# Attention with a decaying complex state and a capacity-limited expert layer: small copies given to GpSimd, constants and first loads placed anew, attention's order planned anew

## The chip, the cores and the metric

One core of a Trainium2 chip runs the whole program. The metric is device time in microseconds (us) from the start of an execution to its end; below it is the median of three runs. The engines are PE (TensorE), DVE (VectorE), ACT (ScalarE), POOL (GpSimd) and SP (SyncE, which here only issues DMA transfers); PEld is PE's weight load.

## The reference

Two layers follow each other. The first is attention with a recurrent state for 4 batches x 8 heads, 768 positions and 48 features; the second sends each of the 3072 tokens to one of 8 experts, 384 tokens each, in the order of the largest logits.

```python
mag = np.sqrt(a_re * a_re + a_im * a_im)
scale = np.minimum(mag, 0.999) / (mag + 1e-06)
a_re_n, a_im_n = (a_re * scale, a_im * scale)
for t in range(S):
    ar, ai = (a_re_n[:, :, t, :, None], a_im_n[:, :, t, :, None])
    new_re = ar * S_re - ai * S_im
    new_im = ar * S_im + ai * S_re
    kv = np.einsum('bhd,bhe->bhde', k[:, :, t], v[:, :, t])
    S_re, S_im = (new_re + kv, new_im)
    y[:, :, t] = np.einsum('bhd,bhde->bhe', q[:, :, t], S_re)
...
logits = x @ w_gate
order = np.argsort(-flat)          # (token, expert) pairs, best first
...                                # a token goes to the first expert that has room
h = np.maximum(x[mask] @ w1[e], 0.0)
out[mask] = h @ w2[e]
```

## The kernel before

**Attention** works on 24 tiles of 128 positions (4 batches x 6). Three tiles make a group; there are 8 groups. The first group is cut into pieces of one and two tiles, the last into pieces of two and one, so that elementwise work on them can begin and end with less data.

For each group `elementwise` turns the decay factors into amounts that a plain product can use. Its stages have short names: F1 and F2 square the real part `ar` and the imaginary part `ai` on ACT, F3 forms `p` from both on DVE, F6 adds the squares on DVE, F5 to F11 take logarithms and exponentials on ACT and products on DVE, S scans the log-magnitude on DVE, G1 and G2 take its exponentials on ACT, G3 and G5 scale `kq` (keys and queries) with them on DVE. A1 and A2 give the angle on ACT, N0 sums it on DVE, T1, T2 and T3 make sine and cosine `CS` on ACT. G4 copies the last column of each tile into `gc` (the gate).

For each tile, `turns` then makes P0 (a copy of that tile's gate from `gc` into column 256 of tile buffer `f`), RQ (on DVE: `f<-kq,CS`, the rotation), and K (six transfers from SP's queue that restack `f` into `KQ`). K waits for both RQ and P0. There are four `f` buffers, so P0 of tile i also waits until K of tile i - 4 has read its buffer, and five `KQ` buffers.

`unit` is the rest of a tile: `kp` turns keys over (PE) and `kt` is its copy (ACT), `sc` are the scores (PE), `am` the masked scores (DVE), `U` the update of the state (PE), `W` the state carried on (DVE), `y` the output (PE), `xT` its copy (ACT), `xp` its turning (PE), `x` the copy of that (ACT), `lg` the logits (DVE). XS stores `x` to DRAM from POOL's queue, for the last two tiles from ACT's. There are two buffers of `x`.

**Fillers.** The table `FILL` gives for each tile a number of matmuls of no use (`sc<-mask,f`), issued ahead of that tile's scores once RQ of the tile is done. Their result is overwritten.

**What sets the order.** Every step is entered with `op` as engine, a cost in us, a priority and what it depends on. `in_order` is a planner in the program: it plays these steps through with one clock per engine and gives out the order of the instructions. Priorities are the tile's number plus an offset by kind of step from the table `OFF`. The class `Queue` then ties the instructions of each engine in that order, so engines run in order, and each waits where the result it needs is late. What is recorded through `Queue` shows as L138 in the profile (one helper line); L279 is ACT's load of a table of functions.

**Constants** are issued ahead of attention, not through `Queue`, so that DVE's constants (`ident`, `mask` at L61 and L62, two copies into `pick` at L83) may stand anywhere between its other instructions. Seven steps `later` (constants of the router, all made by POOL) are entered as DVE steps of 0.87 us each.

**After attention** `Router` and `experts` choose tokens by bisection of a threshold, gather them and run the experts' matmuls (`acc`). This part of the program isn't edited.

Of the kernel before, what the change touches and what calls it, by code (L numbers as in the profile page):

```python
# [15 lines left out]
OP = mybir.AluOpType  # L16
# [34 lines left out]
def constants(nc, con, z, w_gate):  # L51
    v, g = nc.vector, nc.gpsimd

    def t(n, shape, dt=F32):
        x = con.tile(shape, dt, name=n)
        setattr(z, n, x)
        return x

    jp = t("jp", [128, 128], I32)
    g.iota(jp, pattern=[[1, 128]], base=0, channel_multiplier=-1)  # L60
    v.tensor_scalar(t("ident", [128, 128]), jp, 0.0, None, op0=OP.is_equal)  # L61
    v.tensor_scalar(t("mask", [128, 128]), jp, 0.0, None, op0=OP.is_ge)  # L62
# [12 lines left out]
    t("wd", [128, 8])  # L75
    t("cidx", [128, NT])
    t("cidx2", [128, NT, 2], BF)
    t("pid", [128, 1])
    pick = t("pick", [128, 4, 112])
    v.memset(pick, 0.0)  # L80
    for s in range(2):
        r = slice(64 * s, 64 * s + 48)
        v.tensor_copy(pick[r, :, 48 * s:48 * s + 48], z.ident[r, None, r].to_broadcast([48, 4, 48]))  # L83
        g.dma_start(pick[r, :, 96:104], w_gate[:, s].rearrange("p d e -> d p e"))
    for s in range(2):
        r = slice(64 * s, 64 * s + 48)
        g.tensor_scalar(pick[r, :, 104:112], pick[r, :, 96:104], -1.0, None, op0=OP.mult)
    t("lg2", [128, NT + 1, 2, E])
    z.lg = z.lg2[:, :NT, 0]
    t("top", [128, NT])  # L90
    t("qm", [128, NT])
    t("oh", [128, NT, E], BF)
    t("ext", [128, 2])
# [164 lines left out]
def attention(nc, real, tc, z, kq_in, a_re, a_im, v_tok, xd, later):  # L258
    ctx = ExitStack()
    con = ctx.enter_context(tc.tile_pool(name="acon", bufs=1))  # L260
# [5 lines left out]
    v, g = nc.vector, nc.gpsimd  # L266
# [15 lines left out]
    act = nc.scalar.activation  # L282
# [52 lines left out]
    def free(name, stages, gi):  # L335
        return [x for s in stages for x in last_of(s, gi - BUFS[name])]
# [4 lines left out]
    def load_a(gi, j, name, src):  # L341
        b, c0, n = GROUPS[gi]
        lo, hi = cuts[gi][j]
        w = slice(lo * 128, hi * 128)
        return lambda: nc.sync.dma_start(
            get(name, gi, p=ld, bufs=1)[:, :, w], src[b, c0 // GC, :, :, w])

    def load_kq(gi):
# [15 lines left out]
    def elementwise(gi, j, at):  # L364
        b, c0, _ = GROUPS[gi]
        lo, hi = cuts[gi][j]
        n = hi - lo
# [10 lines left out]
        def add(stage, eng, cost, fn, deps):  # L378
            op((stage, gi, j), eng, cost, at, fn, deps)
# [2 lines left out]
            return [(s_, gi, j) for s_ in ss]  # L382

        first = -60.0 + 30.0 * j if gi == 0 else at
        op(("li", gi, j), "dma", 0.6, first, load_a(gi, j, "ai", a_im), free("ai", ["F2", "F3"], gi))
        op(("la", gi, j), "dma", 0.6, first, load_a(gi, j, "ar", a_re), free("ar", ["F1", "F3", "F4"], gi))
        for x in ops[-2:]:
            moved(x, 128 * (1 if n == GC else 3), 12 * T if n == GC else 512 * n)
# [24 lines left out]
        for c in range(n):  # L413
# [7 lines left out]
        add("G2", "act", sca(N3), lambda: act(G_("zi"), G_("zi"), AF.Exp), k_("G1"))  # L421
        add("G3", "dve", dve(N3), lambda: v.tensor_tensor(part(1), part(1), G_("s2").rearrange("p j (c t) -> p c j t", c=n), op=OP.mult),
            k_("G1") + [("lk", gi)])
        add("G4", "dve", 0.075, lambda: v.tensor_copy(
            get("gc", gi, [128, 3, GC], bufs=3)[:, :, lo:hi], G_("s2")[:, :, 127::128]), k_("G1") + free("gc", ["P0"], gi))
        add("G5", "dve", dve(N3), lambda: v.tensor_tensor(part(0), part(0), G_("zi").rearrange("p j (c t) -> p c j t", c=n), op=OP.mult),
            k_("G2") + [("lk", gi)])
# [25 lines left out]
    def turns(i):  # L453
# [8 lines left out]
        def ftile():  # L462
            return tiles["f", i]

        f_free = [("K", i - F_BUFS), ("FI", i - F_BUFS, len(FILL.get(i - F_BUFS, ())) - 1)] if i >= F_BUFS else []
        op(("P0", i), "dve", 0.07, i, lambda: v.tensor_copy(
            ftile()[..., 256], tiles["gc", gi][:, :, c, None].to_broadcast([128, 3, 2])), X("G4") + f_free)
        def rot():
            v.tensor_tensor(ftile()[..., :256].rearrange("p j s (m t) -> p (j s) m t", m=2),
# [159 lines left out]
            load(("lv", gi + 2), 0.6, elementwise_at + 4, load_v(gi + 2),  # L629
                 [("MX", gi * GC + c) for c in range(GC)] + [("ST", gi * GC + c) for c in range(GC)])  # L630
    for n, fn in enumerate(later):
        op(("later", n), "dve", 0.87, NT - 1.0, lambda fn=fn: fn(nc), [("later", n - 1)])

    def choices():
        r = slice(0, NT - 6)
# [46 lines left out]
class Router:  # L682
# [772 lines left out]

# [34 lines left out]
```

## Time and profile before

| what | us |
|---|---|
| median of 3 runs | 508.01 (507.87 to 508.49) |
| the profiled execution, its own time | 503.52 |
| its span, first to last instruction | 501.7 |
| attention: first RQ on DVE starts | 32.34 |
| attention: last `xp` on PE ends | 227.53 |
| PE busy, DVE busy, ACT busy, POOL busy over the span | 447.2, 391.7, 305.6, 113.8 |

The profile comes from one execution; times of rows count from the start of its span. Its own time is 1.8 us longer than its span and 4.5 us shorter than the median of the timed runs. A matmul's end is modelled, so that PE's busy time says that it had something in its queue, not that it ran at its peak. A row with "x8" merges eight equal instructions that follow each other; the time from the start of a row to the start of the next on the same engine is what an instruction costs its engine where no gap is named.

### The profile page before, as it was taken

How to read it: one execution, taken by the hardware profiler on the slowest of the kernel's cores; microseconds unless marked ns; L12 is line 12 of the kernel's file. 1: busy time of each engine (PE TensorE's matmuls, PEld its weight loads, DVE VectorE, ACT ScalarE, POOL GpSimd, SP SyncE). 2: the span in 40 equal slices, each digit the busy share in tenths (PEclk: the TensorE clock that was granted, in tenths of full speed). 3: DMA queues.
4: the chain of work that ended last, by engine and by line, in shares of the span. 5: the costliest groups of instructions: out<-in, count | busy, mean ns of one | idle time of the engine just before them, and what ended most of it. 6: DMA issues, size and time to landing. Idle time of an engine off the chain costs nothing.

```text
span 501.7 us, 9765 instructions
## 1 busy us (share of the span) xinstructions
PE 447.2 (89%) x3659; PEld 385.0 (77%) x3659; DVE 391.7 (78%) x1039; ACT 305.6 (61%) x577; POOL 113.8 (23%) x193
## 2 busy tenths in 40 slices
PE   0029999999999999995489999999999999999996
PEld 0017887888888989994365578898988988999995
DVE  6999999999999999836737778598896978925150
ACT  6999998987998949521033736364473743734241
POOL 8830000000010000012121324150331413830102
PEclk9999999999999999996599999999999999999998
DMA  7718687786879863621352515471170615750001
GB/s 263 303 36 238 196 286 226 240 252 208 253 231 241 249 172 100 168 86 49 127 172 80 220 48 173 159 272 44 54 293 33 258 73 202 286 174 16 33 17 47
DMA packets 37199, 82.51 MB, mean 164 GB/s; under 512 B 4352, under 2 KB 29184, under 8 KB 34080
## 3 DMA queue, kind: packets, MB, share of 16 engines
q1 hardware_dynamic: 30016, 42.55, 28.1%
q0 software_dynamic: 6848, 38.95, 21.3%
q8 instruction: 29, 0.48, 0.4%
q10 hardware_dynamic: 288, 0.39, 0.2%
q14 instruction: 18, 0.15, 0.1%
HBM read 53.49 MB, written 9.44 MB: 125 GB/s over the span
## 4 chain that ended last, share of the span: by engine, by line
PE 52%; DVE 17%; ACT 12%; issue 11%; DMA 4%; POOL 1%; SPq 1%; POOLq 1%; DVEq 0%; ACTq 0%
PE acc L138 35%; ACT s L138 5%; DVE f L138 4%; PE y L138 4%; PE sc L138 4%; PE cnt L138 4%; PE U L138 3%; DVE zi L138 2%; DMA ai<-in_a_im 2%; DVE neg L138 2%; DVE am L138 2%; PE xp L138 2%; DVE p L138 2%; ACT p L138 2%; ACT L279 2%
## 5 line engine op out<-in xcount | busy, mean ns | idle before, releaser
L138 ACT ACTIVATE hh<-acc 128x384 fp32r<-128x384 f32 (+1 forms) x64 | 31.3, 490 | 61.9 <-PE acc L138 54.0
L138 PE MATMUL sc<-mask,f 128*128 128x512 bf16 x126 | 32.4, 398 | 34.1 <-DVE f L138 34.1
L138 ACT ACTIVATE comp<-cnt 32x8 f16<-32x8 f32 (+1 forms) x144 | 24.3, 169 | 57.6 <-PE cnt L138 50.9
L138 PE MATMUL acc<-w2l,hh 128*128 128x384 f32 x168 | 56.7, 350 | 0.0
L138 PE MATMUL acc<-w2h,hl 128*128 128x384 f32 x168 | 56.3, 349 | 0.0
L138 PE MATMUL acc<-w2h,hh 128*128 128x384 f32 x168 | 55.3, 346 | 0.0
L138 PE MATMUL acc<-xh,w1h 128*128 128x384 f32 x168 | 55.0, 347 | 0.0
L138 PE MATMUL acc<-xh,w1l 128*128 128x384 f32 x168 | 54.8, 347 | 0.0
L138 PE MATMUL acc<-xl,w1h 128*128 128x384 f32 x168 | 54.5, 345 | 0.0
L138 POOL DMA_DIRECT2D xd<-x x22 | 12.2, 558 | 182.6 <-ACT x L138 182.5
L138 PEld LDWEIGHTS sc<-KQ 96*128 96x128 f32 x384 | 46.6, 192 | 4.5 <-issue 2.0
L138 PEld LDWEIGHTS <-f 128*128 128x128 bf16 x126 | 12.8, 103 | 48.0 <-DVE f L138 34.1
L138 PE MATMUL sc<-KQ 96*128 96x128 f32 x384 | 48.6, 277 | 0.0
L138 POOL DMA_INDIRECT out<-ot,idx x24 | 24.6, 1026 | 105.3 <-ACT ot L138 97.4
L138 DVE SCALAR_TENSOR_TENSOR hl<-acc,hh 128x384 fp32r<-128x384 f32 x56 | 30.6, 551 | 19.5 <-ACT hh L138 18.7
L138 DVE TENSOR_TENSOR f<-kq,CS 128x1536 f32<-128x1536 f32 x24 | 41.5, 1747 | 0.0
L138 DVE TENSOR_TENSOR ind<-m,thr 128x768 bf16<-128x768 f32 (+1 forms) x45 | 33.9, 771 | 8.5 <-PE thr L138 8.4
L138 POOL DMA_INDIRECT xg<-xd,idx x24 | 30.8, 1283 | 32.2 <-DVE idx L138 12.0
L138 PE MATMUL y<-am,V 128*64 128x128 f32 x384 | 36.5, 278 | 0.0
L138 DVE TENSOR_TENSOR am<-sc,mask 128x512 f32<-128x512 f32 x48 | 31.5, 681 | 5.6 <-PE sc L138 5.6
L138 PEld LDWEIGHTS acc<-w2l,hh 128*128 128x128 f32 x168 | 31.5, 189 | 0.8
L138 PEld LDWEIGHTS acc<-w2h,hl 128*128 128x128 f32 x168 | 31.3, 189 | 0.7 <-issue 0.3
(211 smaller groups left out, 1150.2 us busy)
## 6 DMA issues: line engine op xcount, KB each, us to landing
KQ<-f SPq DMA_DIRECT2D x144, 128.5 KB, 3.0
kq<-in_kq SPq DMA_DIRECT2D x8, 1152.0 KB, 6.6
V<-in_v SPq DMA_DIRECT2D x8, 576.0 KB, 7.5
xd<-x POOLq DMA_DIRECT2D x22, 192.0 KB
ar<-in_a_re SPq DMA_DIRECT2D x6, 576.0 KB, 3.9
ai<-in_a_im SPq DMA_DIRECT2D x6, 576.0 KB, 5.4
ar<-in_a_re SPq DMA_DIRECT2D x2, 384.0 KB, 4.0
ai<-in_a_im SPq DMA_DIRECT2D x2, 384.0 KB, 5.3
```

The source lines that it names most:

```text
L138: r = f(*a, **k)
L279: real.scalar.add_instruction(ins)
```

## The change

- G4 and P0, 10 and 24 small copies, are issued to POOL and no longer to DVE. The planner is given 0.45 and 0.75 us for them.
- The seven `later` steps are entered as POOL steps with costs of their own.
- Constants go through `Queue`, so they stand ahead of the first pieces on DVE. The two negations in `pick` move into the router's constants.
- The first group's two loads of `ai` are issued from ACT's queue; the loads of `ar` stay on SP's.
- `START`, `OFF` and `FILL` have new numbers, and the order comes out anew.

```diff
@@ constants
     for s in range(2):
         r = slice(64 * s, 64 * s + 48)
         v.tensor_copy(pick[r, :, 48 * s:48 * s + 48], z.ident[r, None, r].to_broadcast([48, 4, 48]))
         g.dma_start(pick[r, :, 96:104], w_gate[:, s].rearrange("p d e -> d p e"))
-    for s in range(2):
-        r = slice(64 * s, 64 * s + 48)
-        g.tensor_scalar(pick[r, :, 104:112], pick[r, :, 96:104], -1.0, None, op0=OP.mult)
@@ load_a
-        return lambda: nc.sync.dma_start(
+        q = nc.scalar if gi == 0 and name == "ai" else nc.sync
+        return lambda: q.dma_start(
             get(name, gi, p=ld, bufs=1)[:, :, w], src[b, c0 // GC, :, :, w])
@@ elementwise
-        op(("li", gi, j), "dma", 0.6, first, load_a(gi, j, "ai", a_im), free("ai", ["F2", "F3"], gi))
+        op(("li", gi, j), "dma" if gi else "act", 0.6, first - (0 if gi else 2000.0), load_a(gi, j, "ai", a_im), free("ai", ["F2", "F3"], gi))
...
-        add("G4", "dve", 0.075, lambda: v.tensor_copy(
+        add("G4", "pool", 0.45, lambda: g.tensor_copy(
             get("gc", gi, [128, 3, GC], bufs=3)[:, :, lo:hi], G_("s2")[:, :, 127::128]), k_("G1") + free("gc", ["P0"], gi))
@@ turns
-        op(("P0", i), "dve", 0.07, i, lambda: v.tensor_copy(
+        op(("P0", i), "pool", 0.75, i, lambda: g.tensor_copy(
             ftile()[..., 256], tiles["gc", gi][:, :, c, None].to_broadcast([128, 3, 2])), X("G4") + f_free)
@@ attention
-        op(("later", n), "dve", 0.87, NT - 1.0, lambda fn=fn: fn(nc), [("later", n - 1)])
+        op(("later", n), "pool", LATER[n], NT - 1.0, lambda fn=fn: fn(nc), [("later", n - 1)])
...
-START = dict(pe=0.0, act=0.6, dve=1.5, pool=3.4, dma=0.65)
+LATER = [3.3, 6.7] + [2.8] * 5
+START = dict(pe=0.0, act=0.3, dve=2.6, pool=4.3, dma=0.65)
...
-FILL = {0: (6, 6, 6), 1: (2, 2, 2), 3: (6, 6, 6), 4: (3, 3, 3), 5: (2, 2, 2), 6: (5, 5, 5), 7: (2, 2, 2), 8: (4, 4, 4), 9: (4, 4, 4), 11: (1, 1, 1), 12: (4, 4, 4), 14: (1, 1, 1), 18: (2, 2, 2)}
+FILL = {0: (6, 6, 6), 1: (2, 2, 2), 2: (4, 4, 4), 3: (2, 2, 2), 5: (6, 6, 6), 7: (4, 4, 4), 8: (1, 1, 1), 9: (3, 3, 3), 10: (1, 1, 1), 11: (3, 3, 3), 12: (3, 3, 3), 13: (2, 2, 2)}
@@ Router.masks
+        for s in range(2):
+            r = slice(64 * s, 64 * s + 48)
+            g.tensor_scalar(z.pick[r, :, 104:112], z.pick[r, :, 96:104], -1.0, None, op0=OP.mult)
@@ the program
-    constants(nc, con, z, w_gate)
+    queue = Queue(tc, nc, CHAIN)
+    constants(queue, con, z, w_gate)
     router = Router(nc, z, con)
-    queue = Queue(tc, nc, CHAIN)
```

`FILL` sums to 126 matmuls before and 111 now.

**The front, on DVE.** DVE's rows around its constants, before (`s_217` holds squares, `s_209` the real part's, `gc` and `f_119` are the gate copies of tile 0):

```order
L138 TENSOR_TENSOR s_217<-s_217,s_209 128x3x256
L61 TENSOR_SCALAR ident<-jp 128x128
L62 TENSOR_SCALAR mask<-jp 128x128
L83 COPY pick<-ident 48x4x48 x2
L138 TENSOR_TENSOR p<-p,s_209 128x3x128
L138 SCALAR_TENSOR_TENSOR zi<-zi,s_217 128x128 x3
L138 TENSOR_SCALAR zi<-s_217 128x3x256
L138 COPY gc<-s_217 128x3
L138 COPY f_119<-gc 128x6
```

The start of DVE's queue now:

```order
L135 TENSOR_SCALAR ident<-jp 128x128
L135 TENSOR_SCALAR mask<-jp 128x128
L135 MEMSET cb 128x1 x5
L135 MEMSET pick 128x448
L135 COPY pick<-ident 48x4x48 x2
L135 TENSOR_SCALAR neg<-ar 128x3x128
L135 SCALAR_TENSOR_TENSOR p<-ar,ai 128x3x128
```

The constants moved ahead of the first instruction that needs loaded data, and the copies left DVE. (The helper line is L135 in the changed program.)

**The front, on ACT.** ACT's rows up to the sines and cosines of the first group, before. The piece of one tile is 128x3x128, the piece of two 128x3x256; `CS<-p` is T3, `CS<-neg` T1, `p<-neg` T2; rows of 128x1152 belong to later groups:

```order
L138 ACTIVATE p<-neg 128x3x256
L138 ACTIVATE zi<-zi 128x3x256
L138 ACTIVATE s_280<-s_280,cb 128x1152
L279 ACT_TABLE_LOAD
L138 ACTIVATE CS<-p,cb 128x3x128
L138 ACTIVATE CS<-p,cb 128x3x256
L138 ACTIVATE CS<-neg 128x3x128
L138 ACTIVATE CS<-neg 128x3x256
L138 ACTIVATE s_347<-ai 128x1152
```

The same place now (`s_313` and `s_332` belong to the third group):

```order
L135 ACTIVATE zi<-zi 128x3x256
L135 ACTIVATE s_313<-ar,cb 128x1152
L135 ACTIVATE s_255<-s_255,cb 128x1152
L276 ACT_TABLE_LOAD
L135 ACTIVATE s_332<-ai 128x1152
L135 ACTIVATE CS<-neg 128x3x128
L135 ACTIVATE CS<-neg 128x3x256
L135 ACTIVATE p<-neg 128x3x128
L135 ACTIVATE CS<-p,cb 128x3x128
L135 ACTIVATE p<-neg 128x3x256
L135 ACTIVATE CS<-p,cb 128x3x256
```

Both squares of the third group now stand ahead of the first group's sines; T2 and T3 of the longer piece stand behind the T3 that tile 0 needs.

**The middle, on POOL.** POOL's rows from the last of the router's constants on, before:

```order
L138 TENSOR_TENSOR steps<-sb,sa 2x32
L138 MEMSET weight 128x1
L138 DMA xd<-x 128x384 x22
L138 MEMSET ind_2501 128x96
```

The same place now (groups 1 to 4; `f_117` to `f_120` are the four buffers):

```order
L135 MEMSET weight 128x1
L135 COPY gc<-s_255 128x9
L135 COPY f_120<-gc 128x6
L135 COPY f_117<-gc 128x6
L135 COPY f_118<-gc 128x6
L135 COPY gc<-s_332 128x9
L135 COPY f_119<-gc 128x6
L135 COPY f_120<-gc 128x6
L135 COPY f_117<-gc 128x6
L135 DMA xd<-x 128x384 x3
L135 COPY gc<-s_602 128x9
L135 COPY f_118<-gc 128x6
```

The stores of tiles, which POOL issued as each came, now stand in threes behind four copies of a later group.

**The late middle, on PE.** PE's rows at tile 15 before (`KQ_127` is tile 14, `KQ_123` tile 15):

```order
L138 MATMUL sc<-KQ_127 128x128 x8
L138 MATMUL kp<-ident,KQ_123 128x96 x8
L138 MATMUL sc<-KQ_123 128x128 x4
L138 MATMUL y<-am,V_115 64x128 x2
L138 MATMUL y<-KQ_127,W_111 64x128 x2
```

And now (`KQ_125` is tile 14, `KQ_121` tile 15):

```order
L135 MATMUL y<-am,V_113 64x128 x2
L135 MATMUL y<-KQ_125,W_109 64x128 x2
L135 MATMUL kp<-ident,KQ_121 128x96 x8
L135 MATMUL sc<-KQ_121 128x128 x8
L135 MATMUL kp<-ident,KQ_122 128x96 x8
```

The output `y` of tile 14 now stands ahead of the first use of tile 15 and no longer behind it; six fillers of tile 18, further back, are gone.

## Rows read from the trace of the kernel before

**Rows 1.** Windows: us, busy us (count) by engine, clock, DMA share, GB/s

```profile
34.00:162.00 128.00, 126.45 (x1196) 103.21 (x1196) 125.99 (x192) 115.65 (x137) 7.39 (x13) 1.00 0.78 234
162.00:228.00 66.00, 65.33 (x722) 60.07 (x723) 52.42 (x103) 40.04 (x65) 6.33 (x21) 1.00 0.55 154
```

**Rows 2.** Chain that ended last, 150 to 170: start, us, what

```profile
151.69 1.67 DVE f L138
...
163.96 1.91 PE y L138 x32
```

**Rows 3.** Timeline of PE: start, us, instruction, idle before and its releaser

```profile
34.14 6.09 PE L138 MATMUL sc<-mask,f 128*128 128x512 bf16 x18 [34.14 <-DVE f L138]
...
162.19 0.85 PE L138 MATMUL kp<-ident,KQ 96*128 96x96 f32 x8 [1.02 <-DMA KQ<-f]
...
181.88 1.46 PE L138 MATMUL sc<-mask,f 128*128 128x512 bf16 x6
183.17 1.04 PE L138 MATMUL xp<-pick,xT 112*128 112x112 f32 x8
...
225.49 2.04 PE L138 MATMUL xp<-pick,xT 112*128 112x112 f32 x16
```

**Rows 4.** Timeline of ACT in the front, columns as in group 3

```profile
6.51 0.94 ACT L138 ACTIVATE s<-ar,cb 128x768 f32<-128x768 f32 x1 [0.59 <-DMA ar<-in_a_re]
...
26.41 0.83 ACT L138 ACTIVATE p<-neg 128x768 f32<-128x768 int32 x1
...
30.43 1.44 ACT L138 ACTIVATE CS<-p,cb 128x384 f32<-128x384 f32 x2
31.78 1.24 ACT L138 ACTIVATE CS<-neg 128x384 f32<-128x384 int32 x2
32.93 1.15 ACT L138 ACTIVATE s<-ai 128x1152 f32<-128x1152 f32 x1
```

**Rows 5.** Timeline of DVE, columns as in group 3

```profile
7.67 0.96 DVE L138 SCALAR_TENSOR_TENSOR p<-ar,ai 128x768 f32<-128x768 f32 x1 [0.47 <-DMA ai<-in_a_im]
...
10.01 0.24 DVE L61 TENSOR_SCALAR ident<-jp 128x128 f32<-128x128 int32 x1
...
10.83 0.56 DVE L138 TENSOR_TENSOR p<-p,s 128x384 f32<-128x384 f32 x1
...
32.34 5.08 DVE L138 TENSOR_TENSOR f<-kq,CS 128x1536 f32<-128x1536 f32 x3
...
42.82 1.28 DVE L138 TENSOR_TENSOR am<-sc,mask 128x512 f32<-128x512 f32 x2
44.01 0.16 DVE L138 COPY gc<-s 128x9 f32<-128x9 f32 x1
44.21 0.43 DVE L138 COPY f<-gc 128x6 f32<-128x6 f32 x2
44.56 1.35 DVE L138 TENSOR_TENSOR kq<-kq,s 128x1152 f32<-128x1152 f32 x1
45.82 0.55 DVE L138 TENSOR_TENSOR W<-U,KQ 96x384 f32<-96x384 f32 x1
...
69.06 0.23 DVE L138 COPY f<-gc 128x6 f32<-128x6 f32 x2
69.20 1.35 DVE L138 TENSOR_TENSOR kq<-kq,s 128x1152 f32<-128x1152 f32 x1
```

**Rows 6.** Timeline of DVE at group 6, its gate copy and first rotation

```profile
171.94 0.16 DVE L138 COPY gc<-s 128x9 f32<-128x9 f32 x1
...
176.03 1.75 DVE L138 TENSOR_TENSOR f<-kq,CS 128x1536 f32<-128x1536 f32 x1
```

**Rows 7.** Timeline of POOL in the front; DVE's products into `s`: ns min/median/max

```profile
5.58 0.43 POOL L138 COPY open<-wd 128x8 f32<-128x8 f32 x1
...
19.35 1.53 POOL L138 TENSOR_SCALAR sb<-sb,row 2x32 f32<-2x32 f32 x1
...
L138 DVE TENSOR_TENSOR s<-s,s x10: 554/1345/1400, 6.0 to 161.1; 128x1152 f32<-128x1152 f32 x6, 128x384 f32<-128x384 f32 x2, 128x768 f32<-128x768 f32 x2
```

More of the change, by code (lines that the diff above doesn't have):

```diff
@@ L672 @@
 DMA_DONE = 1.1
-START = dict(pe=0.0, act=0.6, dve=1.5, pool=3.4, dma=0.65)
-OFF = {"A1": 10.983, "F1": 12, "F10": 9.889, "F11": 0.357, "F2": -5.131, "F3": 7.764, "F4": 6.685, "F5": 6.077, "F6": -7.894, "F7": -6.843, "F8": -4.85, "F9": -10.87, "FL": 5.883, "FL<": 2.265, "FN": 8.109, "G1": 2.847, "G2": 10.407, "G3": 4.24, "G4": 0.759, "G5": 6.781, "K": -3.661, "KC": -4.05, "LR": 4.171, "MK": -1.389, "MX": -3.739, "N0": 9.959, "N1": -5.987, "N2": -4.948, "P0": -12, "R0": -4.984, "R1": -0.563, "R2": -1.381, "R3": 8.0, "R4": 7.75, "R5": -6.743, "S": 8.397, "SC": 6.191, "SC<": 7.201, "ST": 2.118, "ST<": -0.224, "T1": -4.411, "T2": 6.329, "T3": -10.754, "TL": -5.903, "UA": 3.009, "UA<": 7.158, "WM": -4.85, "XC": -6.968, "XC<": -0.91, "XE": 1.974, "XS": 5.168, "la": 0.606, "later": 6.458, "li": 9.242, "lk": 0.241, "lv": 11.155, "RK": -3.095, "RQ": -3.878, "table": -7.639, "CA": -1.771, "BE": 9.686, "FI": 6.628, "FI<": -4.723, "A2": -5.288, "la<": -6.631, "li<": 0.611}
+LATER = [3.3, 6.7] + [2.8] * 5
+START = dict(pe=0.0, act=0.3, dve=2.6, pool=4.3, dma=0.65)
+OFF = {"A1": 10.399, "A2": -9.822, "BE": 0.131, "CA": -2.118, "F1": -1.107, "F10": 3.443, "F11": 7.184, "F2": -0.925, "F3": 5.421, "F4": 5.223, "F5": -4.22, "F6": 3.011, "F7": -5.852, "F8": -2.715, "F9": -5.359, "FI": 6.816, "FI<": 9.377, "FL": 9.859, "FL<": -5.873, "FN": 12.915, "G1": 1.011, "G2": -1.21, "G3": -11.062, "G4": -0.449, "G5": -6.433, "K": -5.895, "KC": -14.0, "LR": -0.075, "MK": -7.142, "MX": 7.176, "N0": 3.163, "N2": 4.716, "P0": 12.184, "RQ": 2.776, "S": 7.92, "SC": 10.153, "SC<": -1.898, "ST": 11.563, "ST<": -6.332, "T1": 8.558, "T2": 10.974, "T3": -7.584, "TL": -6.667, "WM": -3.298, "XC": -9.548, "XC<": -8.705, "XE": 10.454, "XS": 9.28, "la": -9.643, "la<": -6.574, "later": 0.869, "li": -8.149, "li<": -7.975, "lk": -3.51, "lv": -2.528, "table": -8.414}
 CHAIN = ("scalar", "vector", "tensor", "gpsimd", "sync")
 F_BUFS, KC_BUFS = 4, 5
-FILL = {0: (6, 6, 6), 1: (2, 2, 2), 3: (6, 6, 6), 4: (3, 3, 3), 5: (2, 2, 2), 6: (5, 5, 5), 7: (2, 2, 2), 8: (4, 4, 4), 9: (4, 4, 4), 11: (1, 1, 1), 12: (4, 4, 4), 14: (1, 1, 1), 18: (2, 2, 2)}
+FILL = {0: (6, 6, 6), 1: (2, 2, 2), 2: (4, 4, 4), 3: (2, 2, 2), 5: (6, 6, 6), 7: (4, 4, 4), 8: (1, 1, 1), 9: (3, 3, 3), 10: (1, 1, 1), 11: (3, 3, 3), 12: (3, 3, 3), 13: (2, 2, 2)}
 SQ = ()
```

## The prediction

> **What bounds the kernel now.** I read the windows of attention first, then the chain that ended last, then the timelines of PE, ACT and DVE. Attention is the only part that the change edits, so the question is when its last matmul ends; it ends at 225.49 + 2.04 = 227.53 [rows 3]. From 34 to 162 both PE (126.45 of 128.00 us) and DVE (125.99) are full [rows 1]. From 162 to 228 PE alone is full (65.33 of 66.00) while DVE is at 52.42 [rows 1]. Between the two stretches stands one wait that both sides can be read from: PE's `kp` of tile 15 begins at 162.19 after 1.02 us without work, released by the transfers of `KQ` [rows 3]. Those follow the rotation of tile 15, which DVE started at 151.69 [rows 2]. So DVE sets the pace up to there, by little, and PE sets it afterwards. In the front, before the first rotation at 32.34 [rows 5], ACT sets it: it runs from 6.51 to the sines of tile 0 at 31.78 [rows 4], and the first rotation starts where the sine of its piece ends.
>
> PE's fullness is partly made. 126 of its matmuls are fillers. Six of them take from 181.88 to 183.17, 0.215 us each [rows 3]. Those that stand where PE would otherwise wait cost nothing; those behind 162 are on the path.
>
> **The front: a loss of 1.5 us.** Three edits meet here.
>
> The constants leave a place in DVE's queue where they took from 10.01 to 10.83 [rows 5], 0.82 us, and go where DVE waits for its first data anyway. But DVE isn't what tile 0 waits for, so I give this nothing. The six-column copies of the front are counted at nothing for the same reason.
>
> The loads of `ai` are issued by ACT beside those of `ar`. The second `ai`, the last of the four pieces, landed just before 7.67, where DVE's product waited for it [rows 5]; the second `ar` landed before 6.51, where ACT began its gapless run [rows 4]. In the new order ACT's run begins with the second `ai` and has the same instructions before it and after it. I put its landing at 6.7: an estimate, between 6.2 (one place earlier than the second `ar` did) and 7.67 (no gain, if the transfers' rate and not their issue sets it). That starts the run 0.2 us later than before.
>
> Inside the run the order differs. Two squares of the third group, 128x1152 each, now stand ahead of the sines; such a square takes 1.15 [rows 4], so 2.3. T1 of the longer piece comes ahead as well: both pieces took from 31.78 to 32.93 [rows 4], and the longer has two thirds of the columns, 0.75. Behind now stand T2 of the longer piece (0.83) and its T3 (30.43 to 31.78 for both pieces, 0.85 for the longer) [rows 4]. 2.3 + 0.75 - 0.83 - 0.85 = 1.4 us more. With the landing, the first rotation and PE's first matmul come 1.6 later; ACT may stand still less than it did, so I take 1.5, with 0.7 and 2.6 as ends (landing at 6.2 with a few tenths saved; landing at 7.67).
>
> **DVE from tile 0 to tile 15: a gain of 3.2.** Between these two rotations DVE loses 5 copies into `gc` and 15 into `f`. One into `gc` costs 0.20 (44.01 to 44.21). Two into `f` cost 0.14 (69.06 to 69.20) or 0.35 where the second waits for its buffer (44.21 to 44.56) [rows 5]. That gives 1.0 + (1.05 to 2.6); I take 2.6 in all, since the waiting kind is the rarer. The product of squares of the third group moves ahead of tile 0, where ACT hides it: a product of this size takes 1.26 (44.56 to 45.82). One update of `W` (0.55) falls behind tile 15 and two masks (1.19 for both, 42.82 to 44.01) come ahead of it [rows 5]. Sum: -2.6 - 1.26 - 0.55 + 1.19 = -3.2. The rotation of tile 15 then starts 1.5 - 3.2 = 1.7 earlier, and if its transfers take as long as before, `kp` of tile 15 could begin at 160.5.
>
> **PE: ready at 162.7, then 3.2 shorter.** Before, PE had done all ahead of tile 15 at 162.19 - 1.02 = 161.17 [rows 3]. Of the 126 fillers 120 stood ahead; now all 111 do. Nine fewer are 1.9 us. `y` of tile 14 now stands ahead of tile 15 too, 1.91 [rows 2], so the two cancel, and with the later start PE is ready at 161.17 + 1.5 = 162.7 if each of its small waits comes again. Behind that point PE took 227.53 - 162.19 = 65.3 us; it now has one `y` (1.9) and six fillers (1.3) less: 62.1.
>
> So attention ends between 160.5 + 62.1 = 222.6, if the earlier transfers remove PE's waits, and 162.7 + 62.1 = 224.8, if none goes: 4.9 or 2.7 us earlier. PE full for 126.45 of 128.00 us [rows 1] speaks for the later end, that a modelled busy PE hides waits speaks against it. I take **3.5 us**. Router and experts, which follow with the same code, move as a whole. The span goes from 501.7 to 498.2, the profiled execution's own time from 503.52 to 500.0, and the median, which stood 4.5 us above that execution, from 508.01 to **504.5**. With the front's ends (0.7 and 2.6 in place of 1.5) the same sum gives 502.3 to 506.4.
>
> **POOL's new work is costed at nothing**, because POOL was busy 7.39 of 128.00 us there [rows 1]. No row shows the copies on POOL. The nearest is a copy of 128x8, 0.43 us; a tiny POOL instruction took up to 1.53 [rows 7]. The place with least cover is group 6, where the gate was copied at 171.94 and the first rotation started at 176.03 [rows 6], ending 1.67 later: 5.8 us. POOL needs two copies by then, 0.9 to 3.1 us. The stores that now stand in threes behind four copies come late by 1.7 to 6.1; a tile's second successor on ACT waits for them, and two buffers of `x` give it a tile's time, some 8.1 us (24 tiles in 227.53 - 34.14 us [rows 3]).
>
> **Rivals.** *POOL holds DVE up (slower).* If a POOL copy stops DVE's two-input products for its whole length, 29 copies behind tile 0 (8 and 21) at 0.43 are 12.5 us on DVE; less the gain of 3.5 that is 9 slower, 517.0. It decides from 0.12 us per copy on (3.5 / 29). Against it: of ten two-input products into `s`, the first of which ran beside POOL's constants and the later ones beside an idle POOL, the longest took 1400 ns where the median is 1345 [rows 7], 0.055 more. Chance 0.08. The Trainium skill ("SBUF — State Buffer", section "SBUF: two separate sides") has it the other way: VectorE and GpSimd share a port pair as an exclusive lock, and whichever starts first, a GpSimd instruction or a VectorE one with two SBUF inputs, blocks the other for its whole length. By that rule this rival would be the likeliest and the time up to 517.0; the row above shows no such length, though few POOL instructions there read much.
>
> *The new order waits more (no change, or a little slower).* Engines run in a fixed order, and DVE idled only 128.00 - 125.99 = 2.0 us from 34 to 162 [rows 1]. If the masks that now come earlier wait for their scores and DVE idles 4.9 more, the rotation of tile 15 comes 4.9 - 1.7 = 3.2 late, PE's shorter rest (3.2) just makes up for it, and all is given back: 508.0; with 7.4 more it is 510.5. For it: PE starts later and the scores of the first tiles with it. Chances 0.13 for within 0.2% and 0.11 for slower.
>
> *The copies don't leave the path (the change doesn't do what it says).* If POOL's copies take 2.9 us each, `K` waits for P0 and not for the rotation; 3.5 us late at one group gives 508.0. The 1.53 of [rows 7] speaks against it; its chance is within the 0.13.
>
> **Chances and range.** The forecast and its neighbours, faster by more than 0.2% (1.0 us, about what a measurement of this kernel can tell from no change): 0.68. Within 0.2%: 0.13. Slower: 0.19. The likeliest case alone gives 502.3 to 506.4. To hold the time 8 times in 10 the range takes in no change and the smaller slower cases, and a bit below the forecast's own end for copies that cost DVE the dearer 0.18 each: 501.5 to 509.0.
>
> **What would show it.** Right: the first rotation near 33.8, PE's first filler near 35.7; that of tile 15 near 150; last `xp` ending near 224; no `gc` or `f` copies on DVE; products on DVE of unchanged length; gaps ahead of `xd` stores on POOL without a wait on ACT for `x` buffers. Wrong: DVE products beside POOL copies longer by tenths; SP's transfers of `KQ` released by POOL; ACT's gapless run starting after 7; more idle time of DVE ahead of masks than 2 us; an end of attention that moved while router and experts did not move with it.

## The result, and the profile after

| | before | after |
|---|---|---|
| median, us | 507.94 (504.78 to 508.49, 4 executions) | 500.22 (498.71 to 500.55, 4 executions) |
| ratio | 1 | 0.9871 (0.9828 to 0.9914) |
| profiled execution, own time | 503.52 | 500.43 |
| first RQ on DVE starts | 32.34 | 33.65 |
| RQ of tile 15 starts (DVE's timeline) | 151.61 | 150.06 |
| `kp` of tile 15 starts | 162.19 | 161.75 |
| last `xp` of attention ends | 227.53 | 223.98 |

The change makes the kernel 1.3% faster, 7.7 us. The forecast was 504.5, within 501.5 to 509.0; the time lies below that range. Between the two profiled executions the difference is only 3.1 us. (The table takes tile 15's rotation from DVE's timeline; the 151.69 of [rows 2] is its place in the chain.)

PE's timeline after, to be read against [rows 3] (start, us, instruction, idle before and its releaser):

```profile
35.51 7.01 PE L135 MATMUL sc<-mask,f 128*128 128x512 bf16 x18 [35.51 <-DVE f L135]
...
161.43 0.39 PE L135 MATMUL y<-KQ,W 96*64 96x128 f32 x4
161.75 0.88 PE L135 MATMUL kp<-ident,KQ 96*128 96x96 f32 x8
...
221.94 2.04 PE L135 MATMUL xp<-pick,xT 112*128 112x112 f32 x16
```

PE begins 1.37 us later, comes to tile 15 0.44 earlier and ends attention 3.55 earlier. The `kp` of tile 15 has no idle time ahead of it any more: the wait of 1.02 for `KQ` is gone, and `y` of tile 14 runs up to it. The windows after, as in [rows 1]:

```profile
34.00:162.00 128.00, 126.49 (x1222) 103.74 (x1223) 126.55 (x173) 116.46 (x139) 27.78 (x36) 1.00 0.77 235
162.00:228.00 66.00, 62.88 (x694) 57.34 (x693) 52.22 (x106) 39.52 (x64) 13.93 (x32) 0.98 0.53 157
```

POOL (the fifth pair) went from 7.39 to 27.78 us in the first stretch, DVE stayed full. The clock of 0.98 in the second belongs to its end: PE is done with attention at 223.98, and the clock is 1.00 from 162 to 224. The front, ACT's timeline after, to be read against [rows 4]:

```profile
6.80 0.84 ACT L135 ACTIVATE s<-ai 128x768 f32<-128x768 f32 x1 [0.75 <-DMA ai<-in_a_im]
...
30.25 1.16 ACT L135 ACTIVATE s<-ai 128x1152 f32<-128x1152 f32 x1
31.32 1.24 ACT L135 ACTIVATE CS<-neg 128x384 f32<-128x384 int32 x2
...
33.00 0.61 ACT L135 ACTIVATE CS<-p,cb 128x384 f32<-128x384 f32 x1
```

And DVE's, where [rows 5] and [rows 2] have 32.34 and 151.69:

```profile
33.65 5.20 DVE L135 TENSOR_TENSOR f<-kq,CS 128x1536 f32<-128x1536 f32 x3 [0.38 <-ACT CS L135]
...
150.06 1.75 DVE L135 TENSOR_TENSOR f<-kq,CS 128x1536 f32<-128x1536 f32 x1
```

The chain that ended last went from 52% PE and 17% DVE to 71% and 3%. In the new kernel it stays on PE from the first filler at 35.51 to tile 15 and beyond, where before it came from DVE's rotation at 151.69 over the transfers of `KQ`.

### The profile page after: what moved, and what is told of

Same layout as the page of the kernel before. It is cut to its first block, busy times and chain, and to the rows that moved or that the text cites. A ratio compares the mean times of both kernels' runs of the same rounds, so it can differ in the third digit from the quotient of the medians.

```text
span 498.6 us, 9821 instructions
## 1 busy us (share of the span) xinstructions
PE 444.0 (89%) x3644; PEld 382.3 (77%) x3644; DVE 389.0 (78%) x1005; ACT 305.6 (61%) x577; POOL 140.9 (28%) x227
## 4 chain that ended last, share of the span: by engine, by line
PE 71%; issue 14%; ACT 6%; DVE 3%; DMA 3%; POOL 2%; POOLq 1%; ACTq 0%; DVEq 0%
PE acc L135 29%; PE sc L135 14%; PE y L135 8%; PE U L135 8%; PE xp L135 4%; PE cnt L135 3%; PE kp L135 3%; ACT s L135 2%; DMA w1t<-in_w,eidx 2%; POOL out L135 2%; DMA ai<-in_a_im 1%; ACT L276 1%; ACT p L135 1%; DVE ind L135 1%; DVE f L135 1%
## 5 line engine op out<-in xcount | busy, mean ns | idle before, releaser
L135 ACT ACTIVATE hh<-acc 128x384 fp32r<-128x384 f32 (+1 forms) x64 | 31.3, 490 | 62.0 <-PE acc L135 54.1
L135 PE MATMUL sc<-mask,f 128*128 128x512 bf16 x111 | 29.3, 412 | 35.5 <-DVE f L135 35.5
L135 ACT ACTIVATE comp<-cnt 32x8 f16<-32x8 f32 (+1 forms) x144 | 24.2, 168 | 57.7 <-PE cnt L135 50.8
L135 PE MATMUL acc<-w2l,hh 128*128 128x384 f32 x168 | 56.7, 350 | 0.0
L135 PE MATMUL acc<-w2h,hl 128*128 128x384 f32 x168 | 56.3, 349 | 0.0
L135 PE MATMUL acc<-w2h,hh 128*128 128x384 f32 x168 | 55.3, 346 | 0.0
L135 PE MATMUL acc<-xh,w1h 128*128 128x384 f32 x168 | 55.1, 347 | 0.0
L135 PE MATMUL acc<-xh,w1l 128*128 128x384 f32 x168 | 54.8, 347 | 0.0
L135 PE MATMUL acc<-xl,w1h 128*128 128x384 f32 x168 | 54.5, 345 | 0.0
L135 POOL DMA_INDIRECT out<-ot,idx x24 | 24.3, 1012 | 106.5 <-ACT ot L135 97.0
L135 PEld LDWEIGHTS <-f 128*128 128x128 bf16 x111 | 10.8, 105 | 49.1 <-DVE f L135 35.5
L135 PE MATMUL sc<-KQ 96*128 96x128 f32 x384 | 48.1, 277 | 0.0
L135 DVE SCALAR_TENSOR_TENSOR hl<-acc,hh 128x384 fp32r<-128x384 f32 x56 | 30.6, 552 | 19.6 <-ACT hh L135 18.7
L135 PEld LDWEIGHTS sc<-KQ 96*128 96x128 f32 x384 | 45.1, 192 | 0.8 <-issue 0.7
L135 DVE TENSOR_TENSOR f<-kq,CS 128x1536 f32<-128x1536 f32 x24 | 41.6, 1750 | 1.0 <-ACT CS L135 0.5
L135 DVE TENSOR_TENSOR ind<-m,thr 128x768 bf16<-128x768 f32 (+1 forms) x45 | 33.9, 771 | 8.4 <-PE thr L135 8.4
L135 POOL DMA_DIRECT2D xd<-x x22 | 13.3, 604 | 93.6 <-ACT x L135 93.6
L135 POOL DMA_INDIRECT xg<-xd,idx x24 | 30.2, 1259 | 32.2 <-DVE idx L135 12.0
L135 DVE TENSOR_TENSOR am<-sc,mask 128x512 f32<-128x512 f32 x48 | 31.9, 680 | 6.8 <-PE sc L135 6.3
L135 PE MATMUL y<-am,V 128*64 128x128 f32 x384 | 36.5, 278 | 0.0
L135 PEld LDWEIGHTS acc<-w2l,hh 128*128 128x128 f32 x168 | 31.5, 189 | 0.7
L135 PEld LDWEIGHTS acc<-w2h,hl 128*128 128x128 f32 x168 | 31.3, 189 | 0.6 <-issue 0.3
```

What stands on the lines that cost most here:

```text
L135: r = f(*a, **k)
```

## The experiments

18 runs. Ratios are to the kernel before on the same chip and occasion, with a 95% interval; bare numbers behind an expectation are the median and the range in us. A theory's letter means what the expectation beside it says. The "granted clock" of an execution is its mean over the span, 1.00 being 2.4 GHz.

**Both kernels once more** (no edit).

> The kernel before, unchanged, timed against itself. Theory A (where a run took place sets the level, not the kernel): its runs on this chip lie within 1 us of each other, and the profiled execution of before (503.52) and its three timed runs (507.87 to 508.49) were simply not taken under the same conditions; ratio 1.000. Theory B (before has a slower course that it takes in some executions): its runs here spread over two levels, near 503.5 and near 508, and a profile of a slow one shows a stretch some 4.5 us longer than in the profile of before.

Before: 504.72 (502.73 to 512.39, 12 executions), ratio 1.0001 (0.9967 to 1.0035).

> The changed kernel, unchanged. Theory A: beside the runs of before on the same chip it is 3.1 to 3.6 us faster, as the two profiles stand to each other (spans 501.7 and 498.6): ratio 0.993 within 0.002. Theory B: ratio 0.987 to 0.990, because before takes its slower course and this kernel does not. Attention's last matmul ends near 224.0, as in the first profile of this kernel.

After: 499.91 (499.37 to 501.46, 6 executions), 0.9904 (0.9872 to 0.9935). So the kernel before does not agree with itself: over the five occasions of these experiments 107 executions took 502.4 to 512.4, median 505.06. They spread over that range with no two levels to be told apart, so neither Theory A (within 1 us) nor Theory B came as said. Of the kernel after, all 16 lie between 498.7 and 501.5; its ratio lies between A's and B's, a little nearer B's. This trace, of its longest execution (501.46), ends attention at 226.07 and not near 224.0; the one of e17 ends it at 224.17.

**The copies alone, and all but the copies.** First, after's order with the copies issued to DVE again:

```diff
-        add("G4", "pool", 0.45, lambda: g.tensor_copy(
+        add("G4", "pool", 0.45, lambda: v.tensor_copy(
...
-        op(("P0", i), "pool", 0.75, i, lambda: g.tensor_copy(
+        op(("P0", i), "pool", 0.75, i, lambda: v.tensor_copy(
```

> The changed kernel with its 34 gate copies issued on DVE again, at the places that the planner gave them on POOL; all other orders as in the changed kernel. Theory P (PE bounds attention from tile 15 on and nearly everywhere before, and DVE's relief only removes slack): at most 1 us slower than the changed kernel, end of attention 224 to 225. Theory D (DVE's 3.7 us of copies are the gain): 2.6 to 3.7 us slower, the rotation of tile 15 near 152.7 and the end of attention near 227.

500.38 (499.53 to 501.8), 0.9913 (0.988 to 0.9945): within 0.5 us of after beside it. From the first rotation to that of tile 15 it took 150.58 - 34.42 = 116.16 us, after 116.41: in this order the copies cost DVE nothing that shows, as Theory P has it (DVE is busy 127.55 us from 34 to 162 instead of 126.55, so they took what it had left). Then before's order with the same two copies on POOL:

> The kernel before with its 34 gate copies issued on POOL, and nothing else changed. Theory P: 1.0 to 1.5 us faster than before (the wait of 1.02 us at tile 15 and little else; its 126 fillers still fill PE). Theory D: 2.6 to 3.7 us faster. If POOL's copies come late for the transfers of KQ it is slower than before, and SP's wait list names POOL.

502.2 (501.62 to 504.47, 12 executions), 0.9957 (0.9932 to 0.9982). By the ratio that is 2.2 us faster, between the two theories. Between the two rotations 118.15 us instead of 119.27 (before's, 32.34 to 151.61 in DVE's timeline), but PE still waits 0.72 for tile 15, and attention ends at 227.68, no earlier than before's 227.53. Its longer executions are gone all the same.

**Looking at longer executions of before** (no edit).

> The kernel before once more, to catch in a trace one of its longer executions. Of its runs so far those at a mean granted clock of 0.974 to 0.980 took 502.5 to 505.9 us, those at 0.965 to 0.973 took 506.7 to 512.4. Theory C (DVE paces PE up to tile 15 without slack; in some executions DVE or a transfer comes late, PE stands still, and its granted clock falls to 1.2 GHz inside attention): in a trace of 507 us or more, the windows of attention from 34 to 228 show a clock under 1.00, and the last xp of attention ends 3 us or more later than 227.5 to 227.9. Rival R (the lateness lies in router or experts): attention ends at 227.5 to 228.5 and the stretch behind it is longer. A run of 502 to 505 tells nothing.

> As the look before it: theory C puts the lateness of an execution of 507 us or more into attention, with a granted clock under 1.00 between 34 and 228 and an end of attention at 230 or later; rival R puts it behind attention. A run of 502 to 505 tells nothing.

> The kernel before. Theory C: an execution of 506 us or more shows a wait of 1.5 us or more ahead of kp of tile 15 and a granted clock under 1.00 between 162 and 194, one of 502 to 504 a wait of about 1 us and 1.00 throughout. Rival R: long executions with the wait at 1 us and attention's end at 227.5 to 228, longer behind it.

> The kernel before; as the look before it: theory C ties the time to the wait ahead of kp of tile 15 and to the granted clock between 34 and 228, rival R to the stretch behind attention.

Six traces of before now exist. Each line is worked out from the timelines of DVE and PE; "landing" is from the end of tile 15's rotation to the start of its `kp`:

| own time | RQ 15 starts | landing | PE's wait | clock, 162 to 194 | `kp` 15 to end of attention | end |
|---|---|---|---|---|---|---|
| 502.55 | 151.70 | 8.78 | 0.96 | 1.00 | 65.34 | 227.56 |
| 502.93 | 152.20 | 8.62 | 0.81 | 1.00 | 65.35 | 227.92 |
| 503.52 | 151.61 | 8.83 | 1.02 | 1.00 | 65.34 | 227.53 |
| 504.99 | 153.01 | 8.66 | 0.85 | 1.00 | 65.34 | 228.76 |
| 506.35 | 152.13 | 10.20 | 2.25 | 0.95 | 66.94 | 231.01 |
| 510.84 | 153.32 | 10.50 | 2.71 | 0.89 | 68.50 | 234.07 |

The clock is that of the window from 162 to 194. In the longest, PE's timeline reads:

```profile
160.91 1.95 PE L138 MATMUL sc<-KQ 96*128 96x128 f32 x16
165.57 1.51 PE L138 MATMUL kp<-ident,KQ 96*128 96x96 f32 x8 [2.71 <-DMA KQ<-f]
166.88 1.97 PE L138 MATMUL sc<-KQ 96*128 96x128 f32 x8
...
169.68 0.64 PE L138 MATMUL y<-am,V 128*64 128x128 f32 x4
170.11 0.64 PE L138 MATMUL y<-KQ,W 96*64 96x128 f32 x4
...
174.42 1.05 PE L138 MATMUL sc<-KQ 96*128 96x128 f32 x8
```

and its windows (the clock is the third number from the end):

```profile
162.00:166.00 4.00, 1.29 (x11) 1.13 (x10) 3.45 (x7) 2.79 (x4) 0.00 (x0) 0.92 0.84 228
166.00:168.00 2.00, 2.00 (x13) 2.00 (x11) 0.15 (x1) 1.37 (x3) 0.00 (x0) 0.50 0.77 192
...
170.00:172.00 2.00, 2.00 (x22) 2.00 (x20) 2.00 (x6) 0.94 (x1) 0.00 (x0) 0.50 0.95 231
172.00:174.00 2.00, 2.00 (x23) 1.66 (x20) 2.00 (x3) 1.54 (x2) 0.00 (x0) 0.94 0.97 401
```

Behind the wait the granted clock is 0.50, that is 1.2 GHz: eight scores take 1.97 instead of 1.05 a little later, four `y` 0.64 where the timeline after, above, has 0.39. PE's busy time looks full all the while (2.00 of 2.00). Against the 502.55 execution the 8.29 us are: rotation of tile 15 later 1.62, landing 1.72, the clock 68.50 - 65.34 = 3.16, behind attention 1.8. Theory C holds for both longer executions; rival R (the lateness behind attention) has about a fifth of it here and a tenth in the other (0.35 of 3.80).

**What stands ahead of those transfers.** SP's queue at tile 15, before:

```profile
149.90 1.25 SPq L138 DMA_DIRECT2D ar<-in_a_re  x2
151.20 1.27 SPq L138 DMA_DIRECT2D ai<-in_a_im  x2
153.39 12.20 SPq L138 DMA_DIRECT2D KQ<-f  x18
```

and after:

```profile
144.36 0.59 SPq L135 DMA_DIRECT2D ar<-in_a_re  x1
...
146.33 0.61 SPq L135 DMA_DIRECT2D ai<-in_a_im  x1
151.84 12.78 SPq L135 DMA_DIRECT2D KQ<-f  x18
```

The issue of the last group's four loads ended 1 us ahead of the first transfer into `KQ`; now it ends 5 us ahead. From issue to landing (least, median, most) these 18 transfers took, in before's profile (view of the tile `KQ`, 148 to 172):

```profile
DMA to landing us min/median/max: 5.0/5.6/6.0
```

and in after's:

```profile
DMA to landing us min/median/max: 2.3/3.5/4.3
```

So before was tried without the loads; the last group's elementwise work then reads the `ar` and `ai` of the group before it, which leaves that part of the computation out:

```diff
+        if gi == 7:
+            return lambda: tiles.update({(name, 7): tiles[name, 6]})
         return lambda: nc.sync.dma_start(
```

> The kernel before without the four loads of ar and ai of the last group (it reads the group before it again), which stand directly ahead of the transfers into KQ of tile 15 in SP's queue. Theory D (those loads crowd the transfers of tile 15, and their landing, 8.6 to 10.2 us after the rotation's end, is what varies): the landing comes 1 to 2 us earlier, PE's wait for KQ of tile 15 goes, the executions above 505 go, median 501 to 503. Rival V (DVE's pace varies, or the lateness is elsewhere): median 504 to 505.5 with the spread of before.

503.88 (502.64 to 506.47, 12 executions), 0.9973 (0.9948 to 0.9999). From issue to landing the median fell from 5.6 to 3.4, PE has no wait for tile 15, no execution shows a clock under 0.974 (5 of before's 17 beside it were under 0.973, and took 506.2 to 510.6). The loads are what makes the transfers late in this order, but the median is above the 501 to 503 expected: the quick executions of before lose nothing to them but a wait of 1 us.

**The clock by itself: work for PE in the wait.** In before, ahead of the first `kp` of tile 15:

```diff
+                    if i == 15 and not hh:
+                        keep(5)
                     kp = ps.tile([128, 4, 96], F32, name="kp", bufs=2)
```

> The kernel before with 5 more fillers (1.07 us) directly ahead of the first kp of tile 15, where PE waits 0.8 to 2.25 us for KQ of tile 15. Theory C (a longer wait there drops the granted clock to 1.2 GHz for some microseconds, which makes the longer executions longer still): the quick executions pay 0 to 0.3 us (502.5 to 504), the executions above 507 mostly go, since PE no longer stands still there; median 503.5 to 504.5, at most one in ten above 507. Rival L (the lateness is that of the transfer alone, the clock has no part in it): same spread as before, 502.5 to 510, median 505. Rival P (PE is full there): 1.07 us slower throughout, median 506.

504.3 (502.85 to 506.62, 12 executions), 0.9984 (0.9959 to 1.0009). All clocks are at 0.974 or more, where 9 of the 23 executions of before beside it were under 0.973; the top came down from 508.8 to 506.6. Two executions of 506.3 and 506.6 remain, at 0.977 and more: lateness without the clock exists too. The sign is theory C's, the size is within the measurement.

**DVE burdened.** In before, the gate copy into `f` three times:

```diff
+            for _ in range(3):
+                v.tensor_copy(ftile()[..., 256], tiles["gc", gi][:, :, c, None].to_broadcast([128, 3, 2]))
```

> The kernel before with the copy of the gate into f done three times on DVE for every tile: 2 x 0.07 to 0.175 us more for each of 24 tiles, 15 of them between the rotations of tile 0 and tile 15: 2.1 to 5.2 us more on DVE there. Theory C (DVE has no slack up to tile 15): attention ends 2 to 5 us later, the median rises by 2 to 6 us to 507 to 511, and more than half of the runs show a granted clock of 0.973 or less. Rival S (PE's fillers leave DVE slack, and the spread of the runs comes from elsewhere): 504 to 505.5 with the same spread.

511.19 (509.88 to 515.1, 6 executions), 1.0106 (1.0063 to 1.0149). In its trace (515.1) it takes 127.03 us between the two rotations, 7.8 more than before and more than the 2.1 to 5.2 expected; PE waits 2.17 and 2.34 us for `KQ` of two tiles, the clock falls behind both, and attention ends at 240.40. DVE has no slack in before's order, against rival S; of the clocks three of six, not more than half, are at 0.973 or less. Then the rotation of tile 15 done twice:

```diff
-        op(("RQ", i), "dve", dve(1536), i, rot, X("T1", "T3", "G3", "G5") + f_free)
+        op(("RQ", i), "dve", dve(1536), i, (lambda: (rot(), rot())) if i == 15 else rot, X("T1", "T3", "G3", "G5") + f_free)
```

> The kernel before with the rotation of tile 15 done twice in a row by DVE (the second writes the same values): 1.68 us later transfers of KQ of tile 15, so that PE's wait there is 2.7 us instead of 1.0 in every execution. Theory C: the wait lengthens by 1.7 us and the granted clock falls behind it in nearly every execution, as in the trace of the 506.35 us execution (2.25 us of wait, 0.61 granted from 164 to 168): attention ends 3 us or more later, no run below 505, median 507 to 509, granted clock 0.974 or less. Rival L (no clock in it): 1.7 us later, median 506.4, fastest 504.2, clocks as before. Rival S (slack behind it): no change.

503.48 (502.49 to 506.75, 12 executions), 0.9977 (0.995 to 1.0004). Theory C failed here: no loss, two executions of twelve above 506. The trace (504.99) shows the wait for `KQ` at 1.04, not 2.7: PE was itself held up, 1.16 us by the masked scores behind the second rotation, and landing took 8.29; the loads stand 2.2 us ahead of the transfers here, which may be why. That a later rotation does not make the usual execution longer stays unexplained, since no quick one of it was traced.

**The fillers.** In after, those behind tile 0 are not issued:

```diff
-            for _ in range(n):
+            for _ in range(0 if i else n):
```

> The kernel after in its own order, but the 93 fillers of tiles 1 to 13 are not issued (their result is never read). Theory P (from tile 0 on PE is what bounds, fillers included): 93 x 0.215 = 20 us of PE's time go, but DVE's own pace then bounds: DVE was busy 126.55 of 128.00 us from 34 to 162, so at most some 2 us can come off; 498 to 500. Theory K (the fillers keep the granted clock at 2.4 GHz): without them PE stands still for 20 us in small waits, the clock falls to 1.2 GHz inside attention, and the time rises by 5 us or more, to 505 or above, with a mean granted clock below 0.96.

506.98 (501.94 to 510.11, 12 executions), clocks 0.941 to 0.964; 7 us lost against after's 499.9 for 20 us of PE's work saved. Theory K holds: in the window from 66 to 98 the clock is 0.73. Two partial cuts, `range(0 if i > 10 else n)` and `range((n + 1) // 2 if i else n)`:

> The kernel after in its own order without the 24 fillers of tiles 11 to 13 (5.2 us of PE). Theory P (PE bounds up to tile 15 as well): PE can be ahead of tile 15 up to 3 us earlier (its KQ could land at about 158.7, rotation start 150.06 and 8.7 us as in the kernel before, where PE now comes to it at 161.75): 497.4 to 499.5. Theory K (the fillers are needed against the clock): PE waits and its granted clock falls within 100 to 170: 501 or more, a wider spread.

> The kernel after in its own order with about half the fillers of tiles 1 to 13 (54 instead of 93; 8.4 us of PE less). Theory P: PE is ahead earlier everywhere and DVE's pace bounds: attention ends 0 to 3 us earlier, 497.4 to 500.4, spread as narrow as after's. Theory K: with half the fillers PE's waits are long enough somewhere between 34 and 130 that the granted clock falls: 501.5 to 506, mean clock 0.95 to 0.97.

500.96 (499.36 to 501.7) and 499.08 (497.08 to 505.34), 6 executions each. Without those of tiles 11 to 13, PE waits 1.21 for `KQ` at 134 and 1.22 for `xT` at 147, the clock is 0.95 from 130 to 162, and nothing is gained on after. That is near Theory K's 501, without its wider spread. Behind the first of these waits the clock stays at 1.00 (134 to 138), around the second it is 0.70 (146 to 150). With half, the median is Theory P's and the spread is K's: the two executions above 504 have clocks of 0.960 and 0.963, and the trace of another has one fall (PE's timeline):

```profile
77.94 1.96 PE L135 MATMUL sc<-KQ 96*128 96x128 f32 x16
82.43 0.64 PE L135 MATMUL y<-am,V 128*64 128x128 f32 x4 [2.53 <-ACT xT L135]
```

So from tile 8 on alone, `range((n + 1) // 2 if i > 7 else n)`, which takes 12 of 39 fillers (2.6 us; the first expectation miscounts them):

> The kernel after in its own order with the fillers of tiles 8 to 13 halved (36 to 21) and all others as they are: 3.2 us of PE less. With all halved, four of six executions took 497.1 to 499.7 and two 505 at a clock of 0.96, and the trace showed the clock fall at 82, at tile 5 or 6. Theory K (each stretch needs its fillers only where PE would stand still for 2 us or more): 497.5 to 500 in nearly all runs, under the 499.9 of after. Rival: PE waits for KQ or xT instead, as without the fillers of tiles 11 to 13, 500 to 501.5.

498.82 (497.92 to 500.04), 0.987 (0.9827 to 0.9914). Beside after on one chip:

> The kernel after, beside e18 on the same chip: 499.4 to 501.5 as before, all executions at a granted clock of 0.973 or more, and in its trace no wait of PE over 0.5 us between 100 and 228.

> The kernel after with 12 of the 39 fillers of tiles 8 to 13 fewer (39 to 27; the expectation of e16 said 36 to 21 and 3.2 us, miscounted: it is 12 fillers, 2.6 us). Theory K: 1 to 2 us under after on the same chip, 498 to 499.5. Rival O (e16's 498.8 was the occasion): the same as after within 0.5 us.

After 499.45 (498.85 to 499.88), 0.9878 (0.985 to 0.9906); with fewer fillers 498.2 (497.08 to 499.96), 0.9859 (0.9828 to 0.989). In the two traces `kp` of tile 15 starts at 162.04 and 160.34, and after's has no wait of PE over 0.5 us between 100 and 228, as expected. The version is likely 1 us quicker than after; six executions each, with intervals that overlap, don't settle it.

## Why the prediction was wrong

- **The front** was right: ACT's run starts at 6.80 (6.7 said), the first rotation comes 1.31 later (1.5 said). Before's run was not quite gapless: it stood still for 0.50 us at 12.49, for DVE's `zi`. That stop is gone, which the text allowed for; from the run's start to the first rotation it took 1.02 us more where 1.4 were reckoned.
- **DVE between the rotations** was right in sum, -2.9 (116.41 against 119.27) for -3.2, and wrong in its working: the copies, entered with -2.6, give about 1 us alone and nothing that shows in the new order. The order gave the rest.
- **PE's end** was right: ready between 160.5 and 162.7, measured 161.75; behind that 62.23 us (62.1 said); attention 3.55 earlier (3.5 said); own time 500.43 (500.0 said). That it fits to 0.05 us is partly luck: the 3.5 was taken between 2.7 and 4.9 with no row that decides, about 0.9 us of PE's small waits went, and the other two traces of after end attention at 226.07 and 224.17.
- **POOL's copies** hid, though not by being short. They ran almost only beside DVE's products into `kq`, whose two inputs are both in SBUF, and hardly beside the rotations. The views of the tiles `gc`, `f` and `kq` after (least, median and most of one, ns), the `kq` lines of before, and one such place in the timelines after:

```profile
L135 POOL COPY f<-gc x24: 188/263/2637, 19.2 to 199.5; 128x6 f32<-128x6 f32 x24
L135 POOL COPY gc<-s x10: 188/508/1977, 18.8 to 198.2; 128x9 f32<-128x9 f32 x6, 128x3 f32<-128x3 f32 x2, 128x6 f32<-128x6 f32 x2
L135 DVE TENSOR_TENSOR f<-kq,CS x24: 1731/1749/1805, 33.6 to 206.8; 128x1536 f32<-128x1536 f32 x24
L135 DVE TENSOR_TENSOR kq<-kq,s x10: 535/1346/1353, 13.1 to 199.3; 128x1152 f32<-128x1152 f32 x6, 128x384 f32<-128x384 f32 x2, 128x768 f32<-128x768 f32 x2
L135 DVE TENSOR_TENSOR kq<-kq,zi x10: 551/1341/1353, 13.6 to 199.8; 128x1152 f32<-128x1152 f32 x6, 128x384 f32<-128x384 f32 x2, 128x768 f32<-128x768 f32 x2
```

```profile
L138 DVE TENSOR_TENSOR kq<-kq,s x10: 548/1347/1350, 14.2 to 204.1; 128x1152 f32<-128x1152 f32 x6, 128x384 f32<-128x384 f32 x2, 128x768 f32<-128x768 f32 x2
L138 DVE TENSOR_TENSOR kq<-kq,zi x10: 554/1346/1350, 14.7 to 204.6; 128x1152 f32<-128x1152 f32 x6, 128x384 f32<-128x384 f32 x2, 128x768 f32<-128x768 f32 x2
```

```profile
168.38 2.89 POOL L135 COPY f<-gc 128x6 f32<-128x6 f32 x3
...
168.34 1.34 DVE L135 TENSOR_TENSOR kq<-kq,s 128x1152 f32<-128x1152 f32 x1
169.61 1.35 DVE L135 TENSOR_TENSOR kq<-kq,zi 128x1152 f32<-128x1152 f32 x1
```

  DVE's rotations were 1733/1748/1753 before. The rival that DVE is stopped by POOL did not come: the longest product into `kq` took 1353 ns after and 1350 before. In the place shown one copy took 2637 ns, from 168.38 to about the end of the second product at 170.96. The Trainium skill ("SBUF — State Buffer", section "SBUF: two separate sides") has whichever of a GpSimd instruction and a VectorE one with two SBUF inputs starts first block the other for its whole length; the trace agrees on POOL's side, and no row shows a product held up by a copy. The other two rivals did not come either. DVE idled 1.45 us from 34 to 162, less than the 2.0 of before, and the waits of SP's queue name DVE's rotations, never POOL:

```profile
SPq L135 <- DVE f L135: 44.0, 6, 17.3
```

- **The step that failed** is the last: "the median, which stood 4.5 us above that execution, from 508.01 to 504.5". It carried before's 4.5 us over to after as if it belonged to both. It belongs to before alone: after's median is 0.2 us below its profiled execution. Even for before, 4.5 was in good part the draw of three executions: over the 107 later executions the median is 505.06, 1.5 us above that execution, and only 12 reach the 507.8 that all three timed runs exceeded. From 505.06 the same 3.5 would have given 501.6, still above the 499.9 and 499.45 measured for after there. Two of the six traces show what the excess is made of where it is large: the transfers of tile 15 land up to 1.9 us later than usual, PE stands still 2.25 or 2.71 us where the profile had 1.02 [rows 3], its clock falls to 1.2 GHz behind that, and a later rotation adds to it. In the new order `KQ` is there before PE is: none of the three traces of after has a wait there. The six transfers of tile 15 are issued from 151.8 to 155.1 and land within 3.7 us of their issue. So all are there by 158.8, an estimate from these numbers, while PE comes at 161.75; a landing 1.9 us later would still reach nobody. The wait was in the rows, and the text priced it at its length in one quick execution.
- **Still open:** on the first occasion three of before's four executions took 507.9 to 508.5. None of these was traced; that they are of the kind seen in the traces of 506.35 and 510.84 is argued from the time alone, and why that occasion drew so many isn't known. Nor is it known why tile 15's rotation itself came 1.6 us later in the longest execution. On the later occasions the gain is 1.0 to 1.2%. How much of the narrower spread is the loads' place and how much DVE's relief isn't divided: taking the loads away, moving the copies, and filling the wait each removed the low clocks by itself.

## What to carry to other kernels

When the profiled execution is much quicker than a median of three, take more executions first, for a part of the difference can be the draw. For the rest, look for a wait of the bounding engine on a transfer that the profile shows short, and price it at what it can become, the clock behind it included. Before carrying a profile's gain onto a median, ask whether the change removes such a wait; then the median gains more than the profile. Fillers earned their time here where PE would otherwise stand still: taking out all behind tile 0 cost 7 us, and taking out a third of those from tile 8 on cost nothing.

## What the runs showed of the hardware

- PE's granted clock fell from 2.4 to 1.2 GHz behind waits of 2.17 to 2.71 us (five of them, in four traces), and not behind the four of 0.81 to 1.02 at tile 15. Without the fillers of tiles 11 to 13 it fell behind a wait of 1.22 and not behind one of 1.21; without any behind tile 0 it was 0.89 from 34 to 66 with no wait above 1.29. So the one wait is not all that counts. The falls at tile 15 cost 1.60 and 3.16 us, beyond the waits themselves. The Trainium skill ("TensorE: Matmul & The Clock Gate", section "HAM oscillation — how this bites in real kernels") tells of a kernel that waits 3 to 5 us for DMA in every step and starts each next step at the lowered clock; the two traces agree, behind shorter waits of 2.25 and 2.71 us.
- The same six transfers took 8.6 to 10.5 us from the rotation's end to their use, in executions of one program (8.78 and 10.20 on one chip, 8.66 and 10.50 on another), with loads issued just ahead of them; without the loads PE did not wait for them.
- A copy of 128x6 on POOL took 188 ns to 2.6 us, while DVE's products beside it kept their length (at most 1353 ns, before 1350).
